# One-token attention over a long cache with a gated feed-forward branch: 28 of 32 tiles put into a hardware loop

## The chip, the cores and the metric

The kernel runs on one core of one Trainium2 chip, as one program without any work on the host. The metric is the device time of that program in microseconds (us); less is better. Timed runs of the kernel before agree within 0.13 us.

## The reference

A decode step: four sequences of one token each, 32 heads of 128, a cache of 4096 keys and values for each head, all in float32.

```
g = sigmoid(sum(x * gate_w))                       # x: 4 x 512, one gate for each sequence
q = x @ wq                                         # 4 x (32 heads x 128)
p = softmax(q . k_cache / sqrt(128))               # k_cache: 4 x 32 x 4096 x 128
a = (p . v_cache) @ wo                             # v_cache as k_cache; wo: 4096 x 512
b = (gelu(x @ w_gate) * (x @ w_up)) @ w_down       # 512 x 1792, 1792 x 512
out = g * a + (1 - g) * b                          # 4 x 512
```

The two caches are 268 MB each; each of their elements is used once.

## The kernel before

The 128 pairs of sequence and head are cut into 32 tiles of four heads of one sequence. Tile `i` has group `g = i // 4` (which four heads) and sequence `b = i % 4`. A tile's keys, K(i), are 128 partitions x 16384 elements, 8.4 MB: 32 partitions for each head, each with 128 keys of 128 elements. Its values, V(i), have the same layout. In the large SBUF buffer `big`, two K places overlap by a quarter of a tile (`RO` rows), and there is one V place; the last V goes to a K place.

All loads are issued by SP, in the order of the program, into one hardware queue. For each tile in a Python loop over `i`, fully unrolled, the order written by hand (`manual_schedule`, the program order is kept on each engine) is:

- DVE: `products(i, True)` and `sums(i, True)` work on the quarter of K(i) that the next K tile will overwrite ("shared"). Then SP may issue K(i+1).
- DVE: `products(i, False)` and `sums(i, False)` on the other three quarters. `products` multiplies K in place with the queries spread over the partitions (`QB`), `sums` adds up 128 elements for each score.
- PE: `pv(i-1)`, 32 matrix products of the weights `PM` of the tile before with V(i-1), into `PO`. Then SP may issue V(i).
- `max_a(i)`: DVE takes the maximum of each partition (L226), PE transposes the column to a row (L228).
- In the next tile, between its shared products and sums, `soft_max(i)`: DVE reduces the row to one maximum for each head (L233), PE spreads it to all partitions with a product with ones (L235), ACT copies it with a scale (L237), and four exponentials on ACT (L240) write `PM` and the row sums `RS`.
- At every fourth tile `gather` collects the four tiles' outputs with matrix products, and `weigh` divides by the row sums and writes to `ONA` with each head's values repeated four times (L300). After 16 tiles, `turn` transposes (L307) and `turned` masks and adds; the same for the second half at the end.
- `q_spread(g)` makes `QB` for a group by four matrix products, one for each head, with a column of `hmask` (L196), once in four tiles.

The gate and the first two products of the feed-forward branch run under tile 0. Behind the last tile SP loads `w_down` and `wo` (in eight pieces), and PE multiplies `wo` by the attended values as the pieces land. `SC` (scores), `m1`, `nb`, `RS` and `QB` have two buffers each.

Of the kernel before, what the change touches and what calls it, by code (L numbers as in the profile page):

```python
# [9 lines left out]
F32 = mybir.dt.float32  # L10
AF = mybir.ActivationFunctionType
OP = mybir.AluOpType
AX = mybir.AxisListType
# [4 lines left out]
def tile_gated_mix(ctx: ExitStack, tc: tile.TileContext, x, kc, vc, wq, wo, w_gate, w_up, w_down, gate_w, out):  # L18
    nc = tc.nc
    P = 128  # L20
    B, H, S, D = kc.shape
    DM = x.shape[2]
# [3 lines left out]
    HT = 4  # L26
# [10 lines left out]
    HW = 16  # L37
    E = HW * D // P
    GW = HW // HT
    WO_END = ((0, E // 2, E), (0, 4, 8, 11, 13, 15, E))  # L40
    scale = 1.0 / math.sqrt(D)
    c_gelu = math.sqrt(2.0 / math.pi)
# [23 lines left out]
    def place(a, n):  # L66
        return big[:, a:a + n]

    def K(i):
        return place(KB_ * (i % 2), TW)  # L70

    def V(i):
        return place(VA if i < NT - 1 else 0, TW)

    def load_kv(src, i, dst):
        nc.sync.dma_start(dst, src[i % B, HT * (i // B):HT * (i // B) + HT].rearrange("h (p r) d -> (h p) (r d)", p=PH))

    def load_k(i):
        load_kv(kc, i, K(i))

    def load_v(i):
        load_kv(vc, i, V(i))

    def load_f(s):
        nc.sync.dma_start(place((F0, F1)[s], KC * F), (w_gate, w_up)[s].rearrange("(p c) n -> p (c n)", c=KC))
# [14 lines left out]
    load_k(0)  # L100
    gw = consts.tile([P, KC], F32)
    nc.sync.dma_start(gw, gate_w.rearrange("(p c) -> p c", c=KC))

# [11 lines left out]

    PZ = RJ * HT
    PM = consts.tile([P, PZ + R // RJ * 32], F32)
    RS = [consts.tile([P, B, HT], F32, name=f"rs{j}") for j in range(2)]
    for t in [PM] + RS:
        nc.vector.memset(t, 0.0)  # L120


    xT_ps = ps2.tile([P, KC, B], F32, name="sm")
# [46 lines left out]
    hmask = consts.tile([P, 4, HG], F32)  # L170
# [4 lines left out]
    nc.vector.tensor_reduce(bmask, m16.rearrange("p (j b) -> p b j", b=B), axis=AX.X, op=OP.add)  # L175
    nc.vector.tensor_reduce(pmask, m16.rearrange("p (g h) -> p h g", h=HT), axis=AX.X, op=OP.add)
    nc.vector.tensor_reduce(amask, ident.rearrange("p (m a) -> p a m", a=HG), axis=AX.X, op=OP.add)
    nc.vector.tensor_reduce(hmask, ident.rearrange("p (j b a) -> p j a b", j=4, b=B), axis=AX.X, op=OP.add)
    u = place(VA - 4 * DM, 2 * DM).rearrange("p (s n) -> p s n", s=2)
    qd = place(VA - DM, D)  # L180
    for s in range(2):
# [5 lines left out]
                            op=OP.mult)  # L187


    QB = {}  # L190

    def q_spread(g):
        ps = ps1.tile([P, B, D], F32, name="q")
        for h in range(HT):
            j, a = divmod(HT * g + h, HG)
            nc.tensor.matmul(ps[h * PH:(h + 1) * PH].rearrange("p b d -> p (b d)"),  # L196
                             hmask[:, j, a:a + 1].to_broadcast([P, PH]), QM.rearrange("p b d -> p (b d)"),
                             start=True, stop=True)
        QB[g] = work.tile([P, B, D], F32, name="qb")
        nc.scalar.activation(QB[g], ps, AF.Copy)  # L200


    SC = {}

    def rows(i, shared):

        return ((R - RO, R), (0, R - RO))[not shared] if i % 2 == 0 else ((0, RO), (RO, R))[not shared]

    def products(i, shared):
        g, b = divmod(i, B)  # L210
        r0, r1 = rows(i, shared)
        t = K(i).rearrange("p (r d) -> p r d", d=D)[:, r0:r1]
        nc.vector.tensor_tensor(t, t, QB[g][:, b:b + 1, :].to_broadcast([P, r1 - r0, D]), op=OP.mult)  # L213

    def sums(i, shared):
        if shared:
            SC[i] = work.tile([P, R], F32, name="sc")
        r0, r1 = rows(i, shared)
        nc.vector.tensor_reduce(SC[i][:, r0:r1], K(i).rearrange("p (r d) -> p r d", d=D)[:, r0:r1], axis=AX.X, op=OP.add)  # L219


    MT = {}

    def max_a(i):
        m1 = work.tile([P, 1], F32, name="m1")
        nc.vector.tensor_reduce(m1, SC[i], axis=AX.X, op=OP.max)  # L226
        MT[i] = ps2.tile([1, P], F32, name="sm")
        nc.tensor.transpose(MT[i], m1, ident)  # L228

    def soft_max(i):  # L230
        g, b = divmod(i, B)
        m2 = work.tile([1, HT], F32, name="m2")
        nc.vector.tensor_reduce(m2, MT[i].rearrange("o (h p) -> o h p", h=HT), axis=AX.X, op=OP.max)  # L233
        nbp = ps2.tile([P, HT], F32, name="sm")
        nc.tensor.matmul(nbp, ones[:1, :], m2, start=True, stop=True)  # L235
        nb = work.tile([P, HT], F32, name="nb")
        nc.scalar.activation(nb, nbp, AF.Copy, scale=-scale)  # L237
        for h in range(HT):
            s = slice(h * PH, (h + 1) * PH)
            nc.scalar.activation(PM[:, PZ:].rearrange("p (c m) -> p c m", m=32)[s, :, h:RJ * HT:HT],  # L240
                                 SC[i][s, :].rearrange("p (c j) -> p c j", j=RJ), AF.Exp, bias=nb[s, h:h + 1], scale=scale,
                                 accum_out=RS[g % 2][s, b, h:h + 1])


    acc = ps1.tile([P, C4], F32, name="acc")
# [18 lines left out]
        nc.scalar.activation(t, wide, AF.Copy)  # L264
        project(stack, t, True, False)

    def pv(i):
        b = i % BP
        N, n = RJ * D, R // RJ
        for j in range(n):  # L270
            c, m0 = j % 4, PZ + 32 * j - RJ * HT * b
            nc.tensor.matmul(PO[i // BP % 2][32 * c:32 * c + 32].rearrange("p j d -> p (j d)"), PM[:, m0:m0 + 32],  # L272
                             V(i)[:, j * N:(j + 1) * N], start=b == 0 and j < 4, stop=b == BP - 1 and j >= n - 4)

    O, OS, OT = {}, {}, {}

    def gather_a(i):
        O[i // BP] = work.tile([P, RJ, D], F32, name="o")  # L280
        nc.scalar.activation(O[i // BP], PO[i // BP % 2], AF.Copy)  # L281

    def gather(g):
        OS[g] = ps2.tile([B * HT, D + 1], F32, name="sm")
        N = B // BP
        for n in range(N):
            m0 = BP * HT * (1 - n)
            for j in range(RJ):
                nc.tensor.matmul(OS[g][:, :D], sel[:, j, m0:m0 + B * HT], O[N * g + n][:, j, :],  # L289
                                 start=(n, j) == (0, 0), stop=(n, j) == (N - 1, RJ - 1))  # L290
        nc.tensor.matmul(OS[g][:, D:], RS[g % 2].rearrange("p b h -> p (b h)"), ones[:, :1], start=True, stop=True)  # L291

    ONA = consts.tile([B * HT, E, GW, HT, D // E], F32)

    def weigh(g):
        ri = work.tile([B * HT, 1], F32, name="ri")
        nc.vector.reciprocal(ri, OS[g][:, D:])  # L299
        nc.vector.tensor_scalar(ONA[:, :, g % GW], OS[g][:, :D].rearrange("p (k e) -> p e k", e=E)[:, :, None, :]  # L300
                                .to_broadcast([B * HT, E, HT, D // E]), ri, None, op0=OP.mult)


    def turn(w):
        OT[w] = ps1.tile([P, E, B * HT], F32, name="oT")
        for e in range(E):
            nc.tensor.transpose(OT[w][:, e], ONA[:, e].rearrange("q g h k -> q (g h k)"), ident[:B * HT, :B * HT])  # L307
# [47 lines left out]

    load_f(0)
    load_f(1)
    q_spread(0)
    for i in range(NT):
        g, b = divmod(i, B)  # L360
        products(i, True)
        if i > 0:
            soft_max(i - 1)
        if i > B and b == 1 and g % GW == 0:
            turned(g // GW - 1)
        sums(i, True)
        if i < NT - 1:
            load_k(i + 1)
        else:
            load_v(i)  # L370
        products(i, False)
        if i == 0:
            half, gmask = gates()
            ffn_up(0)
            ffn_up(1)
            ffn_gelu()
            load_v(0)
        sums(i, False)
        if i > 0:
            pv(i - 1)  # L380
            if i < NT - 1:
                load_v(i)
            if i % BP == 0:
                gather_a(i - 1)
            if b == 0:
                gather(g - 1)
        max_a(i)
        if i > 0 and b == 0:
            weigh(g - 1)
            if g % GW == 0:  # L390
                turn(g // GW - 1)
        if b == 1 and g + 1 < NG:
            q_spread(g + 1)
    load_d()
    load_w(0)
    load_w(1)
    spread(0)
    soft_max(NT - 1)
    pv(NT - 1)
    gather_a(NT - 1)  # L400
    gather(NG - 1)
    weigh(NG - 1)
    ffn_down()
    turn(1)
    turned(1)
# [31 lines left out]
```

## Time and profile before

| what | value |
|---|---|
| median of three timed runs | 1313.58 us (1313.56 to 1313.69) |
| span of the profiled execution, first to last instruction | 1311.7 us |
| time of the profiled execution outside its span | not listed; the timed median lies 1.9 us above the span |
| instructions | 6366 |
| busy share: PE, DVE, ACT | 30%, 87%, 7% |
| data moved | 565 MB at a mean of 431 GB/s |
| mean granted TensorE clock | 0.633 |

In the rows of the profile that are shown below, a line such as `L213` is a line of the kernel before, and `out<-in` names the buffers. In a timeline row the first number is the start in us from the start of the span, the second the duration in us; in square brackets stand the idle time of that engine just ahead and what ended it. In a row of a group the numbers behind the bar are busy time in us, the mean duration of one in ns, and again the idle time ahead. `SPq` rows are the issues of transfers. A matrix product in float32 appears as two records, so the 32 products of `pv` are shown as 64.

### The profile page before, as it was taken

What the parts mean: (1) busy time and instruction counts of PE and PEld (TensorE: products, weight loads), DVE (VectorE), ACT (ScalarE), POOL (GpSimd) and SP (SyncE); (2) the same over time, 40 slices, a digit from 0 to 9 for tenths busy, and PEclk for the clock granted to TensorE, in tenths of its full rate; (3) what the DMA queues carried; (4) which work ended last, traced back from release to release, by engine and by line L of the source; (5) the groups of instructions that cost most, each with busy time, mean ns of one, the idle gap of its engine ahead of it and who ended that gap; (6) DMA issues with size and microseconds to landing.
All of it is one profiled execution on the core that took longest, in us unless ns stands there. A gap on an engine that the chain in (4) does not pass through costs nothing.

```text
span 1311.7 us, 6366 instructions
## 1 busy us (share of the span) xinstructions
PE 392.2 (30%) x2728; PEld 131.1 (10%) x2728; DVE 1143.1 (87%) x261; ACT 92.6 (7%) x321; POOL 0.7 (0%) x6
## 2 busy tenths in 40 slices
PE   2403323322233221333232233322133333123237
PEld 0100001000010000100001000100001000010013
DVE  1899889988899988988989988998889898898890
ACT  0010000000000100000000000000000000000010
POOL 0000000000000000000000000000000000000000
PEclk9656666556666655666656666665566665566669
DMA  9999999999999999999999999999999999999998
GB/s 416 436 428 442 422 440 426 438 436 436 436 428 436 432 436 436 436 430 432 434 436 434 436 430 436 428 438 430 434 446 422 442 422 442 434 434 440 426 426 341
DMA packets 11143, 565.07 MB, mean 431 GB/s; under 512 B 1368, under 2 KB 1384, under 8 KB 1900
## 3 DMA queue, kind: packets, MB, share of 16 engines
q1 hardware_dynamic: 11116, 564.68, 99.5%
q8 instruction: 21, 0.34, 0.1%
q14 instruction: 6, 0.05, 0.0%
HBM read 564.67 MB, written 0.01 MB: 430 GB/s over the span
## 4 chain that ended last, share of the span: by engine, by line
DMA 73%; DVE 26%; issue 0%; PE 0%; SPq 0%; ACT 0%; DVEq 0%
DMA big<-in_A_k_cache 69%; DVE big L213 13%; DVE sc L219 13%; DMA big<-in_A_v_cache 2%; DMA big<-in_A_wo 2%; DVE m L233 0%; DVE hT L349 0%; PE acc L259 0%; DVE big L346 0%; DVE big L345 0%; DVE big L341 0%; DVE big L343 0%; ACT big L344 0%; DVE m L226 0%; DVE t L313 0%
## 5 line engine op out<-in xcount | busy, mean ns | idle before, releaser
L213 DVE TENSOR_TENSOR big<-big,qb 128x4096 f32<-128x4096 f32 x64 | 555.8, 8685 | 104.1 <-DMA big<-in_A_k_cache 104.1
L219 DVE TENSOR_REDUCE sc<-big 128x32 f32<-128x4096 f32 x64 | 555.4, 8678 | 1.1
L272 PE MATMUL po<-big,PM 128*32 128x512 f32 x2048 | 295.1, 741 | 437.2 <-DMA big<-in_A_v_cache 434.8
L272 PEld LDWEIGHTS po<-big,PM 128*32 128x32 f32 x2048 | 80.9, 133 | 625.2 <-issue 622.7
L235 PE MATMUL sm<-m,ones 1*128 1x4 f32 x64 | 18.7, 360 | 218.0 <-DVE m L233 218.0
L228 PE MATMUL sm<-ident,m 128*1 128x128 f32 x32 | 11.7, 365 | 214.5 <-DVE m L226 182.7
L240 ACT ACTIVATE PM<-sc,nb 32x128 f32<-32x128 f32 x128 | 67.3, 526 | 2.5
L237 ACT ACTIVATE nb<-sm 128x4 f32<-128x4 f32 x32 | 5.5, 173 | 570.3 <-PE sm L235 570.3
L235 PEld LDWEIGHTS sm<-m,ones 1*128 1x128 f32 x64 | 15.9, 306 | 237.7 <-DVE m L233 237.7
L281 ACT ACTIVATE o<-po 128x512 f32<-128x512 f32 x16 | 9.6, 597 | 324.8 <-PE po L272 324.8
L228 PEld LDWEIGHTS sm<-ident,m 128*1 128x1 f32 x32 | 2.5, 79 | 237.0 <-issue 185.9
L240 ACT ACTIVATION_READ_ACCUMULATOR PM<-sc,nb 32x1 f32 x128 | 26.2, 205 | 0.0
L200 ACT ACTIVATE qb<-q 128x512 f32<-128x512 f32 x8 | 4.8, 597 | 245.3 <-PE q L196 245.3
L128 DVE COPY xT<-sm 128x128 f32<-128x128 f32 x4 | 0.9, 284 | 20.6 <-PE sm L125 20.6
L196 PE MATMUL q<-QM,hmask 128*32 128x512 f32 x64 | 14.6, 1004 | 3.5 <-DVE QM L186 3.5
L289 PE MATMUL sm<-o,sel 128*16 128x128 f32 x128 | 15.6, 273 | 0.0
L334 PE MATMUL q<-big,xT 128*32 128x448 f32 x64 | 10.3, 810 | 9.4 <-DMA big<-in_B_w_gate 4.9
L299 DVE RECIPROCAL ri<-sm 16x1 f32<-16x1 f32 x8 | 1.2, 146 | 13.3 <-PE sm L291 13.3
L289 PEld LDWEIGHTS sm<-o,sel 128*16 128x16 f32 x128 | 11.8, 97 | 7.4 <-issue 5.0
L413 DVE COPY res<-acc 128x128 f32<-128x128 f32 x1 | 0.3, 291 | 12.7 <-PE acc L259 12.7
L226 DVE TENSOR_REDUCE m<-sc 128x1 f32<-128x128 f32 x32 | 9.2, 286 | 1.1
L233 DVE TENSOR_REDUCE m<-sm 1x4 f32<-1x128 f32 x32 | 8.7, 272 | 0.6 <-PE sm L228 0.6
(61 smaller groups left out, 77.1 us busy)
## 6 DMA issues: line engine op xcount, KB each, us to landing
big<-in_A_wo SPq DMA_DIRECT2D x2, 2048.0 KB, 27.0
big<-in_B_w_gate SPq DMA_DIRECT2D x1, 3584.0 KB, 21.4
big<-in_B_w_up SPq DMA_DIRECT2D x1, 3584.0 KB, 27.5
big<-in_B_w_down SPq DMA_DIRECT2D x1, 3584.0 KB, 18.0
big<-in_A_wo SPq DMA_DIRECT2D x2, 1024.0 KB, 24.6
big<-in_A_wo SPq DMA_DIRECT2D x2, 512.0 KB, 28.2
big<-in_A_wo SPq DMA_DIRECT2D x1, 768.0 KB, 28.0
big<-in_A_k_cache SPq DMA_DIRECT2D x32, 29.6
```

What stands on the lines that cost most here:

```text
L196: nc.tensor.matmul(ps[h * PH:(h + 1) * PH].rearrange("p b d -> p (b d)"), hmask[:, j, a:a + 1].to_broadcast([P, PH]), QM.rearrange("p b d ...
L213: nc.vector.tensor_tensor(t, t, QB[g][:, b:b + 1, :].to_broadcast([P, r1 - r0, D]), op=OP.mult)
L219: nc.vector.tensor_reduce(SC[i][:, r0:r1], K(i).rearrange("p (r d) -> p r d", d=D)[:, r0:r1], axis=AX.X, op=OP.add)
L226: nc.vector.tensor_reduce(m1, SC[i], axis=AX.X, op=OP.max)
L228: nc.tensor.transpose(MT[i], m1, ident)
L233: nc.vector.tensor_reduce(m2, MT[i].rearrange("o (h p) -> o h p", h=HT), axis=AX.X, op=OP.max)
L235: nc.tensor.matmul(nbp, ones[:1, :], m2, start=True, stop=True)
L240: nc.scalar.activation(PM[:, PZ:].rearrange("p (c m) -> p c m", m=32)[s, :, h:RJ * HT:HT], SC[i][s, :].rearrange("p (c j) -> p c j", j=RJ) ...
L272: nc.tensor.matmul(PO[i // BP % 2][32 * c:32 * c + 32].rearrange("p j d -> p (j d)"), PM[:, m0:m0 + 32], V(i)[:, j * N:(j + 1) * N], start ...
L281: nc.scalar.activation(O[i // BP], PO[i // BP % 2], AF.Copy)
L289: nc.tensor.matmul(OS[g][:, :D], sel[:, j, m0:m0 + B * HT], O[N * g + n][:, j, :], start=(n, j) == (0, 0), stop=(n, j) == (N - 1, RJ - 1))
L334: nc.tensor.matmul(ps[32 * j:32 * j + 32, :], xT[:, c, :32], place((F0, F1)[s] + c * F + j * FG, FG), start=c == 0, stop=c == KC - 1)
```

## The change

Tile 0 is run ahead of the loop. Tiles 1 to 28 run in a hardware loop of seven turns on all engines: one turn is four slots, `b` = 1, 2, 3 and 0, the last of them the first tile of the next group. Tiles 29 to 31 are unrolled after it. Each engine counts the turns in a register, computes from it the addresses and the values of semaphores that it waits for, and branches back. There is no barrier between turns. Behind the loop, in the built program, SP waits until the semaphores of all eight load lanes and of PE, ACT and DVE have the values of the last turn, all engines meet in one barrier, POOL clears the loop's eleven semaphores, and the code after the loop begins.

Other edits that come with it:

- The maxima stay on DVE: the column of partition maxima is repeated over 32 columns and transposed in 32x32 blocks, and reduced again with a changed sign. `soft_max(b)` follows `sums(b, False)` in the same slot. The factor 1/sqrt(128) is put into the queries (`bmask`), so that the exponentials use a scale of 1.
- The queries are spread by one matrix product with `hcur`, a copy of four columns of `hmask`, each 32 times, that DVE writes once a turn (`q_pick`).
- `SC`, `m1`, `nb`, `RS` and `QB` have one buffer each.
- `gather` writes the first seven groups to `ON`; `expand` repeats them behind the loop. `expand(0)`, `turn(0)` and `turned(0)` stand behind tile 31, ahead of `pv(31)`.

```diff
-    def load_kv(src, i, dst):
-        nc.sync.dma_start(dst, src[i % B, HT * (i // B):HT * (i // B) + HT].rearrange("h (p r) d -> (h p) (r d)", p=PH))
+    def load_kv(src, g, b, dst):
+        nc.sync.dma_start(dst, src[b, bass.ds(g * HT, HT)].rearrange("h (p r) d -> (h p) (r d)", p=PH))
...
+    nc.vector.tensor_scalar(bmask, bmask, scale, None, op0=OP.mult)
...
+    def q_pick(g):
+        nc.vector.tensor_scalar(hcur, hmask[:, bass.ds(g * HT, HT), None].to_broadcast([P, HT, PH]), 1.0, None, op0=OP.mult)
+
+    def q_spread():
         ps = ps1.tile([P, B, D], F32, name="q")
-        for h in range(HT):
-            j, a = divmod(HT * g + h, HG)
-            nc.tensor.matmul(ps[h * PH:(h + 1) * PH].rearrange("p b d -> p (b d)"),
-                             hmask[:, j, a:a + 1].to_broadcast([P, PH]), QM.rearrange("p b d -> p (b d)"),
-                             start=True, stop=True)
-        QB[g] = work.tile([P, B, D], F32, name="qb")
-        nc.scalar.activation(QB[g], ps, AF.Copy)
+        nc.tensor.matmul(ps.rearrange("p b d -> p (b d)"), hcur.rearrange("p h k -> p (h k)"),
+                         QM.rearrange("p b d -> p (b d)"), start=True, stop=True)
+        nc.scalar.activation(QB, ps, AF.Copy)
...
+    def soft_max(b):
+        nc.vector.tensor_reduce(m1, SC, axis=AX.X, op=OP.max)
+        nc.vector.transpose(mt, m1.to_broadcast([P, PH]))
+        nc.vector.tensor_reduce(nb, mt, axis=AX.X, op=OP.max, negate=True)
         for h in range(HT):
             s = slice(h * PH, (h + 1) * PH)
             nc.scalar.activation(PM[:, PZ:].rearrange("p (c m) -> p c m", m=32)[s, :, h:RJ * HT:HT],
-                                 SC[i][s, :].rearrange("p (c j) -> p c j", j=RJ), AF.Exp, bias=nb[s, h:h + 1], scale=scale,
-                                 accum_out=RS[g % 2][s, b, h:h + 1])
+                                 SC[s, :].rearrange("p (c j) -> p c j", j=RJ), AF.Exp, bias=nb[s], scale=1.0,
+                                 accum_out=RS[s, b, h:h + 1])
...
+        if last:
+            nc.vector.tensor_scalar(OX[:, :, GW - 1], q[:, :, None].to_broadcast([B * HT, E, HT, D // E]), ri, None,
+                                    op0=OP.mult)
+        else:
+            nc.vector.tensor_scalar(ON[:, bass.ds(g, 1)], q[:, None], ri, None, op0=OP.mult)
+
+    def expand(w):
+        for n in range(GW):
+            if w * GW + n < NG - 1:
+                nc.vector.tensor_copy(OX[:, :, n], ON[:, w * GW + n, :, None, :].to_broadcast([B * HT, E, HT, D // E]))
...
+    def slot(g, b, last=False):
+        c = (b - 1) % B
+        gn = g + 1 if b == 0 else g
+        if b == 1:
+            q_pick_next(g)
+        products(b, True)
+        sums(b, True)
+        if not last:
+            load_k(gn if b < B - 1 else g + 1, (b + 1) % B)
         else:
-            load_v(i)
...
+            load_v(g, b, True)
+        products(b, False)
+        sums(b, False)
+        pv(c)
+        if not last:
+            load_v(gn, b)
+        if c % BP == BP - 1:
+            gather_a(c // BP)
+        if b == 0:
+            gather(g)
+        if b == B - 1:
+            q_spread()
+        soft_max(b)
...
+    with tc.For_i(0, NL, iteration_sync="reg_based") as g:
+        for b in (1, 2, 3, 0):
+            slot(g, b)
+    q_pick_next = lambda g: None
+    for b in range(1, B):
+        slot(NG - 1, b, b == B - 1)
     load_d()
     load_w(0)
     load_w(1)
+    expand(0)
+    turn(0)
+    turned(0)
     spread(0)
-    soft_max(NT - 1)
-    pv(NT - 1)
-    gather_a(NT - 1)
-    gather(NG - 1)
-    weigh(NG - 1)
+    expand(1)
+    pv(B - 1, True)
+    gather_a(1)
+    gather(NG - 1, True)
     ffn_down()
```

More of the change, by code (lines that the diff above doesn't have):

```diff
@@ L39, in tile_gated_mix @@
     GW = HW // HT
+    NL = NG - 1
     WO_END = ((0, E // 2, E), (0, 4, 8, 11, 13, 15, E))
@@ L67, in place, with K, V, load_k @@
         return big[:, a:a + n]
[L69 to L73, printed above, removed]
-    def load_kv(src, i, dst):
[L76 to L82, printed above, removed]
+    def K(b):
+        return place(KB_ * (b % 2), TW)
+    def V(last):
+        return place(0 if last else VA, TW)
+    def load_kv(src, g, b, dst):
+        nc.sync.dma_start(dst, src[b, bass.ds(g * HT, HT)].rearrange("h (p r) d -> (h p) (r d)", p=PH))
+    def load_k(g, b):
+        load_kv(kc, g, b, K(b))
+    def load_v(g, b, last=False):
+        load_kv(vc, g, b, V(last))
     def load_f(s):
@@ L99, in tile_gated_mix @@
     nc.sync.dma_start(x_sb, x.rearrange("b s d -> (b s) d"))
-    load_k(0)
+    load_k(0, 0)
     gw = consts.tile([P, KC], F32)
@@ L117, in tile_gated_mix @@
     PM = consts.tile([P, PZ + R // RJ * 32], F32)
-    RS = [consts.tile([P, B, HT], F32, name=f"rs{j}") for j in range(2)]
-    for t in [PM] + RS:
-        nc.vector.memset(t, 0.0)
+    RS = consts.tile([P, B, HT], F32)
+    nc.vector.memset(PM, 0.0)
+    nc.vector.memset(RS, 0.0)
     xT_ps = ps2.tile([P, KC, B], F32, name="sm")
@@ L169, in tile_gated_mix @@
     amask = consts.tile([P, HG], F32)
-    hmask = consts.tile([P, 4, HG], F32)
+    hmask = consts.tile([P, H], F32)
+    hcur = consts.tile([P, HT, PH], F32)
     pmask = consts.tile([P, HT], F32)
@@ L175, in tile_gated_mix @@
     nc.vector.tensor_reduce(bmask, m16.rearrange("p (j b) -> p b j", b=B), axis=AX.X, op=OP.add)
+    nc.vector.tensor_scalar(bmask, bmask, scale, None, op0=OP.mult)
     nc.vector.tensor_reduce(pmask, m16.rearrange("p (g h) -> p h g", h=HT), axis=AX.X, op=OP.add)
     nc.vector.tensor_reduce(amask, ident.rearrange("p (m a) -> p a m", a=HG), axis=AX.X, op=OP.add)
-    nc.vector.tensor_reduce(hmask, ident.rearrange("p (j b a) -> p j a b", j=4, b=B), axis=AX.X, op=OP.add)
+    nc.vector.tensor_reduce(hmask.rearrange("p (j a) -> p j a", j=4), ident.rearrange("p (j b a) -> p j a b", j=4, b=B),
+                            axis=AX.X, op=OP.add)
     u = place(VA - 4 * DM, 2 * DM).rearrange("p (s n) -> p s n", s=2)
@@ L187, in tile_gated_mix @@
                             op=OP.mult)
-    QB = {}
-    def q_spread(g):
+    QB = consts.tile([P, B, D], F32)
+    def q_pick(g):
+        nc.vector.tensor_scalar(hcur, hmask[:, bass.ds(g * HT, HT), None].to_broadcast([P, HT, PH]), 1.0, None, op0=OP.mult)
+    def q_spread():
         ps = ps1.tile([P, B, D], F32, name="q")
-        for h in range(HT):
-            j, a = divmod(HT * g + h, HG)
-            nc.tensor.matmul(ps[h * PH:(h + 1) * PH].rearrange("p b d -> p (b d)"),
-                             hmask[:, j, a:a + 1].to_broadcast([P, PH]), QM.rearrange("p b d -> p (b d)"),
-                             start=True, stop=True)
-        QB[g] = work.tile([P, B, D], F32, name="qb")
-        nc.scalar.activation(QB[g], ps, AF.Copy)
@@ L203, in tile_gated_mix @@
[L203 to L219, printed above, removed]
@@ L222, in tile_gated_mix @@
[L222 to L237, printed above, removed]
+        nc.tensor.matmul(ps.rearrange("p b d -> p (b d)"), hcur.rearrange("p h k -> p (h k)"),
+                         QM.rearrange("p b d -> p (b d)"), start=True, stop=True)
@@ new lines, in q_spread, with rows, products, sums @@
+        nc.scalar.activation(QB, ps, AF.Copy)
+    SC = consts.tile([P, R], F32)
+    def rows(b, shared):
+        return ((R - RO, R), (0, R - RO))[not shared] if b % 2 == 0 else ((0, RO), (RO, R))[not shared]
+    def products(b, shared):
+        r0, r1 = rows(b, shared)
+        t = K(b).rearrange("p (r d) -> p r d", d=D)[:, r0:r1]
+        nc.vector.tensor_tensor(t, t, QB[:, b:b + 1, :].to_broadcast([P, r1 - r0, D]), op=OP.mult)
+    def sums(b, shared):
+        r0, r1 = rows(b, shared)
+        nc.vector.tensor_reduce(SC[:, r0:r1], K(b).rearrange("p (r d) -> p r d", d=D)[:, r0:r1], axis=AX.X, op=OP.add)
@@ L238, in soft_max @@
+    m1 = consts.tile([P, 1], F32)
+    mt = consts.tile([P, PH], F32)
+    nb = consts.tile([P, 1], F32)
+    def soft_max(b):
+        nc.vector.tensor_reduce(m1, SC, axis=AX.X, op=OP.max)
+        nc.vector.transpose(mt, m1.to_broadcast([P, PH]))
+        nc.vector.tensor_reduce(nb, mt, axis=AX.X, op=OP.max, negate=True)
         for h in range(HT):
@@ L265, in fold, with pv, gather_a, gather @@
         project(stack, t, True, False)
-    def pv(i):
-        b = i % BP
+    def pv(b, last=False):
         N, n = RJ * D, R // RJ
         for j in range(n):
[L271 to L284, printed above, removed]
+            c, m0 = j % 4, PZ + 32 * j - RJ * HT * (b % BP)
+            nc.tensor.matmul(PO[b // BP][32 * c:32 * c + 32].rearrange("p j d -> p (j d)"), PM[:, m0:m0 + 32],
+                             V(last)[:, j * N:(j + 1) * N], start=b % BP == 0 and j < 4, stop=b % BP == BP - 1 and j >= n - 4)
+    O = [consts.tile([P, RJ, D], F32, name=f"o{n}") for n in range(B // BP)]
+    def gather_a(n):
+        nc.scalar.activation(O[n], PO[n], AF.Copy)
+    ON = consts.tile([B * HT, NG - 1, E, D // E], F32)
+    OX = place(ES + 2 * E * 32 + DM, E * GW * HT * D // E)[:B * HT].rearrange("q (e g h k) -> q e g h k", e=E, g=GW, h=HT)
+    ri = consts.tile([B * HT, 1], F32)
+    def gather(g, last=False):
+        os_ = ps2.tile([B * HT, D + 1], F32, name="sm")
         N = B // BP
@@ L288, in gather @@
             for j in range(RJ):
-                nc.tensor.matmul(OS[g][:, :D], sel[:, j, m0:m0 + B * HT], O[N * g + n][:, j, :],
+                nc.tensor.matmul(os_[:, :D], sel[:, j, m0:m0 + B * HT], O[n][:, j, :],
                                  start=(n, j) == (0, 0), stop=(n, j) == (N - 1, RJ - 1))
[L291 to L301, printed above, removed]
+        nc.tensor.matmul(os_[:, D:], RS.rearrange("p b h -> p (b h)"), ones[:, :1], start=True, stop=True)
+        nc.vector.reciprocal(ri, os_[:, D:])
+        q = os_[:, :D].rearrange("q (k e) -> q e k", e=E)
+        if last:
[7 more added lines that the diff above has]
+                nc.vector.tensor_copy(OX[:, :, n], ON[:, w * GW + n, :, None, :].to_broadcast([B * HT, E, HT, D // E]))
+    OT = {}
     def turn(w):
@@ L306, in turn @@
         for e in range(E):
-            nc.tensor.transpose(OT[w][:, e], ONA[:, e].rearrange("q g h k -> q (g h k)"), ident[:B * HT, :B * HT])
+            nc.tensor.transpose(OT[w][:, e], OX[:, e].rearrange("q g h k -> q (g h k)"),
+                                ident[:B * HT, :B * HT])
     def turned(w):
@@ L357, in tile_gated_mix, with q_pick_next @@
     load_f(1)
[L358 to L368, printed above, removed]
-        else:
-            load_v(i)
[L371 to L393, printed above, removed]
+    q_pick(0)
+    q_spread()
+    products(0, True)
+    sums(0, True)
+    load_k(0, 1)
+    products(0, False)
+    half, gmask = gates()
+    ffn_up(0)
+    ffn_up(1)
+    ffn_gelu()
+    load_v(0, 0)
+    sums(0, False)
+    soft_max(0)
+    def slot(g, b, last=False):
[7 more added lines that the diff above has]
+            load_k(gn if b < B - 1 else g + 1, (b + 1) % B)
+        else:
+            load_v(g, b, True)
[9 more added lines that the diff above has]
+        if b == B - 1:
+            q_spread()
+        soft_max(b)
+    def q_pick_next(g):
+        q_pick(g + 1)
+    with tc.For_i(0, NL, iteration_sync="reg_based") as g:
[4 more added lines that the diff above has]
+        slot(NG - 1, b, b == B - 1)
     load_d()
```

## The prediction

> **What bounds the kernel now.** I read the page first: its forty slices, the queues and the chain that ended last.
>
> ```profile
> DMA  9999999999999999999999999999999999999998
> GB/s 416 436 428 442 422 440 426 438 436 436 436 428 436 432 436 436 436 430 432 434 436 434 436 430 436 428 438 430 434 446 422 442 422 442 434 434 440 426 426 341
> q1 hardware_dynamic: 11116, 564.68, 99.5%
> q8 instruction: 21, 0.34, 0.1%
> DMA 73%; DVE 26%; issue 0%; PE 0%; SPq 0%; ACT 0%; DVEq 0%
> ```
>
> The transfers are busy in every slice but the last, at a rate that hardly moves: the kernel is bound by the bytes of its one load queue. The chain gives 26% to DVE, which tempts one to save DVE time. Whether that share is real is read from one tile in the timeline (start, duration, engine, line). I take tile 28 and the start of tile 29, where the change puts the end of its loop.
>
> ```profile
> 1134.37 0.33 SPq L76 DMA_DIRECT2D big<-in_A_k_cache  x1
> 1154.47 0.33 SPq L76 DMA_DIRECT2D big<-in_A_v_cache  x1
> 1163.99 4.43 DVE L213 TENSOR_TENSOR big<-big,qb 128x4096 f32<-128x4096 f32 x1 [2.63 <-DMA big<-in_A_k_cache]
> 1168.53 4.41 DVE L219 TENSOR_REDUCE sc<-big 128x32 f32<-128x4096 f32 x1
> 1172.97 0.33 SPq L76 DMA_DIRECT2D big<-in_A_k_cache  x1
> 1183.40 9.08 PE L272 MATMUL po<-big,PM 128*32 128x512 f32 x64 [14.16 <-DMA big<-in_A_v_cache]
> 1192.54 0.33 SPq L76 DMA_DIRECT2D big<-in_A_v_cache  x1
> 1202.71 4.42 DVE L213 TENSOR_TENSOR big<-big,qb 128x4096 f32<-128x4096 f32 x1 [3.60 <-DMA big<-in_A_k_cache]
> ```
>
> K(29) is issued at 1134.37 and V(28) at 1154.47. They land in the order of issue, 19.4 us apart: K(29) starts DVE at 1163.99, V(28) starts PE at 1183.40, K(30) starts DVE at 1202.71. Each issue comes well before the queue runs dry. K(30) is issued at 1172.97, 10.4 us before V(28) lands; V(29) at 1192.54, 10.2 us before K(30) lands. So the DVE pieces in the chain are covered: an issue that comes up to 10 us later costs nothing. What costs time is a gap in the queue.
>
> ```profile
> 165.59 0.33 SPq L76 DMA_DIRECT2D big<-in_A_k_cache  x1
> 1211.68 0.33 SPq L76 DMA_DIRECT2D big<-in_A_k_cache  x1
> 83.24 4.42 DVE L213 TENSOR_TENSOR big<-big,qb 128x4096 f32<-128x4096 f32 x1
> 98.74 8.69 PE L272 MATMUL po<-big,PM 128*32 128x512 f32 x64 [10.27 <-DMA big<-in_A_v_cache]
> 118.26 4.42 DVE L213 TENSOR_TENSOR big<-big,qb 128x4096 f32<-128x4096 f32 x1
> ```
>
> The first two rows are the issues of K(4) and K(31), 27 tiles apart: 38.74 us a tile. The two DVE rows are tiles 1 and 2, where K had long landed and DVE ran without a pause: 35.02 us a tile. DVE has 3.7 us a tile to spare. (The PE row, V(0)'s landing, is for the start, below.)
>
> **Part 1: inside the loop.** The loads keep their bytes, layout and order. DVE loses the reduction of the transposed maxima (L233) and gains a 32x32 transpose and a reduction of 32 columns; once per turn it also writes the 128x128 head selector (`hcur`).
>
> ```profile
> L233 DVE TENSOR_REDUCE m<-sm 1x4 f32<-1x128 f32 x32 | 8.7, 272 | 0.6 <-PE sm L228 0.6
> L349 DVE STREAM_TRANSPOSE hT<-big 128x32 f32<-128x32 f32 x14 | 1.7, 192 | 0.0
> L175 DVE TENSOR_REDUCE bmask<-m 128x4 f32<-128x16 f32 x1 | 0.2, 178 | 0.0
> L128 DVE COPY xT<-sm 128x128 f32<-128x128 f32 x4 | 0.9, 284 | 20.6 <-PE sm L125 20.6
> L300 DVE TENSOR_SCALAR ONA<-sm,ri 16x512 f32<-16x512 f32 x8 | 5.9, 738 | 0.3
> L213 DVEq EVENT_SEMAPHORE  x1: 21/21/21, 42.0 to 42.0; - x1
> L219 DVE TENSOR_REDUCE sc<-big 128x96 f32<-128x12288 f32 x32 | 414.5, 12952 | 1.1
> L213 DVE TENSOR_TENSOR big<-big,qb 128x12288 f32<-128x12288 f32 x32 | 414.2, 12945 | 0.0
> L240 ACT ACTIVATE PM<-sc,nb 32x128 f32<-32x128 f32 x128 | 67.3, 526 | 2.5
> L240 ACT ACTIVATION_READ_ACCUMULATOR PM<-sc,nb 32x1 f32 x128 | 26.2, 205 | 0.0
> ```
>
> Nearest rows: +0.19 for the transpose, +0.18 for the reduction, +0.28/4 for the selector, -0.27: +0.17 us a tile, so 35.2. The unrolled kernel had nearly no register work. The built loop body holds 68 DVE instructions, 31 of them arithmetic; the other 37, 9.2 a slot, compute registers or wait. No row shows a register operation. Bounds: 0.021 us each (the semaphore row) to 0.33 us (SP's load issue), so 0.2 to 3.1 us a slot; I take the low end, as most are of the semaphore's sort and can run under an operation of 13 us. Even the high end gives 38.3, under 38.74. PE and ACT work is shorter or equal (four query matmuls become one; the maxima's transpose, broadcast and copy go). `soft_max` now ends the slot, and its four exponentials need at most 4 x (0.53 + 0.21) = 2.9 us: they end before the next tile's `sums` overwrites the one score buffer, some 8 us on. **Sum inside the loop: 0**, covered by the queue; from below, at most 3.9 us could be won, 27 tiles x (38.74 - 38.60), if every tile took only what tile 28 took (1134.37 to 1172.97).
>
> [...] The trace before has no branch; its instruction queue (q8) moved 0.34 MB with no engine waiting. [...]
>
> **Part 2: the loop's end.** The built program does not flow from turn 7 into tile 29. Behind its last load, V(28), SP waits until all eight load semaphores have their final value, V(28)'s landing included; then all engines meet in a barrier, and only then comes tile 29. Queued behind that wait on SP are K(30) and V(29); behind the barrier, DVE's products of tile 29 and PE's pv(28). Before, K(29) started DVE at 1163.99; now nothing starts until V(28) has landed, 1183.40, with an empty queue.
>
> ```profile
> 0.34 0.10 POOL L426 MEMSET const-uint8-127<- 128x1 uint8 x1
> 0.83 0.17 DVE L106 MEMSET ones<- 128x128 f32 x1 [0.83 <-PEq L426]
> 1309.04 0.66 SPq L414 DMA_DIRECT2D out<-res  x1
> big<-in_A_wq SPq DMA_DIRECT2D x1, 21.9
> ```
>
> - Barrier. The nearest row is the barrier that opens the program: POOL's last memset ends at 0.44, DVE starts at 0.83, 0.4 us. The exit has two such hops and clears eleven semaphores: I take 1.0. Bounds 0.4 and 2.7 (from the output's issue at 1309.04 to the span's end, 1311.7, a store, its landing and the closing barrier together). DVE starts tile 29 at 1184.4.
> - Issue of K(30): after the shared products and sums, 1163.99 to 1172.97, 8.98 us: 1193.4. V(29) follows pv(28), 9.1 us after the barrier: 1193.5, right behind it.
> - Landing of K(30). In a full queue a load takes 19.4; the one load issued to an empty queue, wq, with the same bytes, took 21.9 from issue to landing. K(30) lands at 1215.3, against 1202.7: **+12.6 us**. The cost of starting is between 0 (19.4) and 2.5.
>
> [...]
>
> Afterwards the queue is full again. DVE at 35.3 a tile starts tile 30 at 1219.7 and tile 31 at 1255.0, so K(31) is issued at 1228.7, before V(29) lands at 1234.7, and V(31) at 1264.0, before V(30) lands at 1273.4. V(31) lands at 1292.7. The lost time is not won back: the bytes bound.
>
> **Part 3: the tail.** Expanding and turning the first half moves behind tile 31.
>
> ```profile
> 1279.97 27.61 DMA big<-in_A_wo
> 1280.35 8.39 PE L272 MATMUL po<-big,PM 128*32 128x512 f32 x64 [2.45 <-ACT PM L240]
> 1293.94 1.16 PE L307 MATMUL oT<-ident,ONA 16*128 16x16 f32 x16
> 1298.36 1.92 PE L254 MATMUL wide<-big 128*32 128x512 f32 x16 [1.40 <-DMA big<-in_A_wo]
> 1303.23 1.08 PE L259 MATMUL acc<-big 128*32 128x128 f32 x32 [0.94 <-DMA big<-in_A_wo]
> 1305.06 0.86 PE L259 MATMUL acc<-big 128*32 128x128 f32 x24 [0.75 <-DMA big<-in_A_wo]
> 1306.26 0.65 PE L259 MATMUL acc<-big 128*32 128x128 f32 x16 [0.34 <-DMA big<-in_A_wo]
> 1307.62 1.03 PE L259 MATMUL acc<-big 128*32 128x128 f32 x24 [0.72 <-DMA big<-in_A_wo]
> ```
>
> Tile 31's maxima are ready near 1290.6; four copies of at most 0.74 (L300's row) and sixteen transposes of 1.16 in all stand on PE ahead of pv(31), which starts near 1295.1. Shifted by 12.6 it would have started at 1293.0: 2.1 us late. PE waits for wo pieces by 1.40 + 0.94 + 0.75 + 0.34 + 0.72 = 4.2 us after that, so the last piece still ends the kernel. **Sum: 0**; copies at twice the price make pv(31) 5.1 late, 0.9 us at the end.
>
> The start: K(2), the tightest issue, has 6.5 us of cover (issued 8.96 after tile 1's 83.24; V(0) lands at 98.7). `q_pick` and the entry's register writes fit in it.
>
> **Sum.** Span 1311.7 + 12.6 = 1324.3. The timed runs lie 1.9 above the span (median 1313.58), so 1313.58 + 12.6 = **1326.2 us**.
>
> **Rivals.**
> - **A, not slower: the exit passes early.** If SP's waits were met by an older count, K(30) would be issued as now; the barrier's 1.0 us would vanish in the 10.4 of cover, and the time would be 1313.6, or as low as 1309.7 with the 3.9 of part 1. It decides if K(30) is issued before V(28) lands. Against it: the registers step by 16 a turn and the semaphores start at 16, so the exit's value is met by the seventh V load alone.
> - **B: DVE becomes the bound.** From 0.38 us for a register operation on, a slot exceeds 38.74. At 0.5 it is 39.8, 1.1 x 28 = 31 us more: 1357. For it: nothing shows such an operation. Against it: 34.7 of the 35 us are four long operations (twice 4.4, twice 12.95), under which they can run.
> [...]
>
> **How the numbers follow.** Forecast 0.86; A 0.06 (two thirds without a change, one third faster), B 0.04, C 0.04. A difference under 0.2%, 2.6 us, can't be told from none. Slower: 0.86 + 0.08 = 0.94; same 0.04; faster 0.02. Range: low end, barrier 0.4 and the 3.9 won inside the loop, 12.6 - 0.6 - 3.9 = +8.1: 1321.7. High end, barrier 2.7, tail 0.9 and DVE over the bound by 0.15 us a tile (4.2): 12.6 + 1.7 + 0.9 + 4.2 = +19.4: 1333.0. A, B and C at full size stay outside, 0.14 in all.
>
> **What would show it.** Right: K issues 38.6 to 38.8 us apart through the loop; one gap in the transfers of about 12.6 us, with SP waiting for a V load before it and DVE's shared products first after it; DVE back to back at tile 30; the last wo piece still ending the chain. [...]

## The result and the profile after

| | before | changed |
|---|---|---|
| median of the timed runs | 1313.63 us | 1324.79 us |
| ratio to before, 95% interval | | 1.0083 [1.0072, 1.0095] |
| profiled execution: its time, its span | not listed, 1311.7 us | 1324.56 us, 1322.5 us |

The change makes the kernel 11.2 us slower; 12.6 was forecast. Three parts of the page of the changed kernel answer to those shown of before: the forty slices of transfers, what they moved, and the queues.

```profile
DMA  9999999999999999999999999999999999969998
GB/s 413 443 418 438 439 432 430 438 440 424 436 444 420 440 440 420 440 440 428 434 438 440 424 436 444 420 440 440 420 440 440 428 434 438 440 267 412 444 426 353
q1 hardware_dynamic: 11116, 564.68, 98.7%
q8 instruction: 7, 0.11, 0.0%
```

The bytes are the same. There is one hole, in the 36th slice (267 GB/s, 6 tenths busy): the loop's end. Elsewhere the rate is as before. Something else changed that I had not weighed: 7 instruction fetches instead of 21.

The hole in the timeline of the changed kernel (start, duration, engine, line; tile 28 and on):

```profile
1132.02 0.33 SPq L77 DMA_DIRECT2D big<-in_A_k_cache  x1
1151.46 0.33 SPq L77 DMA_DIRECT2D big<-in_A_v_cache  x1
1181.54 4.42 DVE L215 TENSOR_TENSOR big<-big,QB 128x4096 f32<-128x4096 f32 x1 [22.60 <-SPq L444]
1181.69 9.77 PE L263 MATMUL po<-big,PM 128*32 128x512 f32 x64 [28.50 <-SPq L444]
1190.52 0.34 SPq L77 DMA_DIRECT2D big<-in_A_k_cache  x1
1191.52 0.34 SPq L77 DMA_DIRECT2D big<-in_A_v_cache  x1
1217.05 4.42 DVE L215 TENSOR_TENSOR big<-big,QB 128x4096 f32<-128x4096 f32 x1
1231.86 8.59 PE L263 MATMUL po<-big,PM 128*32 128x512 f32 x64 [40.40 <-DMA big<-in_A_v_cache]
1252.55 4.41 DVE L215 TENSOR_TENSOR big<-big,QB 128x4096 f32<-128x4096 f32 x1
```

K(29) and V(28) are issued as ever. Then DVE stands for 22.60 us and PE for 28.50, both released by SP, and K(30) is issued 39.06 us after V(28), where before it was 18.50. What SP itself waited for at the loop's line:

```profile
SPq L397 <- DMA big<-in_A_v_cache: 19.3, 1, 19.3
SPq L397 <- DMA big<-in_A_k_cache: 9.2, 1, 9.2
```

It waited through K(29)'s landing and then 19.3 us for V(28)'s. That is the exit.

For the next steps the landings are needed themselves. The trace holds, for each load, when each of its 16 DMA engines reported; "landed" is the last report, "spread" the time from the first to the last (us):

```
              before             changed
load       landed  spread     landed  spread
V(0)        98.61    1.7       99.12    2.0
V(28)     1183.27    4.4     1180.86    1.9
K(30)     1202.68    4.5     1212.40    0.7
V(31)     1279.95    4.5     1291.08    2.0
last wo   1308.19    4.6     1318.99    1.8
```

So the 10.8 us between the two spans fall into three parts. Up to V(28) the changed kernel is **2.4 ahead**. From V(28) to K(30) it needs 31.5 us where the kernel before needs 19.4: **12.1 lost**. From there to the last piece of wo another **1.1** is lost. -2.4 + 12.1 + 1.1 = 10.8.

### The profile page after: what moved, and what is told of

Same layout as the page of the kernel before. It is cut to its first block, busy times and chain, and to the rows that moved or that the text cites. A ratio compares the mean times of both kernels' runs of the same rounds, so it can differ in the third digit from the quotient of the medians.

```text
span 1322.5 us, 6803 instructions
## 1 busy us (share of the span) xinstructions
PE 356.4 (27%) x2586; PEld 113.7 (9%) x2586; DVE 1153.1 (87%) x308; ACT 87.6 (7%) x290; POOL 0.7 (0%) x6
## 5 line engine op out<-in xcount | busy, mean ns | idle before, releaser
L215 DVE TENSOR_TENSOR big<-big,QB 128x4096 f32<-128x4096 f32 x64 | 555.9, 8686 | 99.1 <-DMA big<-in_A_k_cache 76.4
L219 DVE TENSOR_REDUCE SC<-big 128x32 f32<-128x4096 f32 x64 | 555.9, 8686 | 4.5
L232 ACT ACTIVATE PM<-SC,nb 32x128 f32<-32x128 f32 x128 | 67.2, 525 | 479.1 <-DVE nb L229 476.4
L232 ACT ACTIVATION_READ_ACCUMULATOR PM<-SC,nb 32x1 f32 x128 | 26.1, 204 | 0.0
L203 ACT ACTIVATE QB<-q 128x512 f32<-128x512 f32 x9 | 5.4, 597 | 272.7 <-PE q L201 272.7
L201 PE MATMUL q<-QM,hcur 128*128 128x512 f32 x18 | 10.2, 648 | 3.6 <-DVE hcur L197 3.6
L227 DVE TENSOR_REDUCE m<-SC 128x1 f32<-128x128 f32 x32 | 9.0, 281 | 0.9
L165 PE MATMUL po<-big,xT 128*32 128x512 f32 x64 | 8.4, 684 | 0.4 <-DVE xT L129 0.4
L228 DVE STREAM_TRANSPOSE mt<-m 128x32 f32<-128x32 f32 x32 | 6.8, 211 | 1.6
L229 DVE TENSOR_REDUCE nb<-mt 128x1 f32<-128x32 f32 x32 | 6.0, 186 | 1.1
## 6 DMA issues: line engine op xcount, KB each, us to landing
big<-in_B_w_down SPq DMA_DIRECT2D x1, 3584.0 KB, 19.3
```

The source lines that it names most:

```text
L165: nc.tensor.matmul(PO[s][32 * j:32 * j + 32].rearrange("p j d -> p (j d)"), xT[:, c, :32], w[:, n0:n0 + HB * D], start=c == 0, stop=c == K ...
L201: nc.tensor.matmul(ps.rearrange("p b d -> p (b d)"), hcur.rearrange("p h k -> p (h k)"), QM.rearrange("p b d -> p (b d)"), start=True, sto ...
L215: nc.vector.tensor_tensor(t, t, QB[:, b:b + 1, :].to_broadcast([P, r1 - r0, D]), op=OP.mult)
L219: nc.vector.tensor_reduce(SC[:, r0:r1], K(b).rearrange("p (r d) -> p r d", d=D)[:, r0:r1], axis=AX.X, op=OP.add)
L227: nc.vector.tensor_reduce(m1, SC, axis=AX.X, op=OP.max)
L228: nc.vector.transpose(mt, m1.to_broadcast([P, PH]))
```

## The experiments

**The loop against the other edits.** The Python loop in place of the hardware loop, all else as changed:

```diff
-    with tc.For_i(0, NL, iteration_sync="reg_based") as g:
+    for g in range(NL):
         for b in (1, 2, 3, 0):
             slot(g, b)
```

> The changed kernel with its loop unrolled again: all other edits stay (maxima on DVE, one query product, single buffers, first half expanded and turned in the tail). Theory: the loop's end alone costs the time (V(29) lands 9.7 us later than before, of which the gap is 12.1 and the loop's faster spacing gives back 2.4 to 2.8), so without the loop 1313.6, between 1313 and 1315, with no gap in the transfers, and the spacing of K loads again near 38.74 with some 17 instruction fetches. Rival 1: the other edits brought the faster spacing; then about 1311, spacing 38.64. Rival 2: the other edits cost time in the tail or in the slots; then above 1316.

Measured: 1313.61 us, ratio 0.9999 [0.9991, 1.0008]. Its page:

```profile
span 1311.7 us, 6100 instructions
q8 instruction: 20, 0.33, 0.1%
```

The whole difference is the loop's. Maxima on DVE, the single query product, the single buffers and the expansion in the tail cost and bring nothing that can be measured, and the fetches are back.

**The place of the cut.** The next tile's shared products and sums moved to the end of a turn:

```diff
+    def head(b):
+        products(b, True)
+        sums(b, True)
...
     def slot(g, b, last=False):
...
-        products(b, True)
-        sums(b, True)
...
         soft_max(b)
+        if not last:
+            head((b + 1) % B)
...
+    head(1)
     with tc.For_i(0, NL, iteration_sync="reg_based") as g:
```

> The changed kernel with the loop's cut moved by one step: the shared products and sums of the next tile stand at the end of a turn, so that K(30) can be issued right behind the barrier. Theory: of the 12.1 us at the exit, 9.0 are the shared products and sums that stand between barrier and issue, 0.6 the barrier, 2.5 the start into an empty queue. So 9.0 less than the changed kernel: 1315.8, between 1315 and 1317; K(30) is issued 0.6 to 0.8 us after V(28) has landed. Rival: the exit costs its 12 us wherever it is cut (code behind the loop to be fetched, counters to be cleared); then 1324.8.

Measured: 1316.36 us, ratio 1.0020 [1.0011, 1.0029]. Its timeline at the exit; V(28) landed at 1180.88:

```profile
1181.53 12.96 DVE L215 TENSOR_TENSOR big<-big,QB 128x12288 f32<-128x12288 f32 x1 [10.99 <-PEq L449]
1181.97 0.34 SPq L77 DMA_DIRECT2D big<-in_A_k_cache  x1
```

DVE now stands 11.0 us instead of 22.6, and K(30) is issued 1.1 us after the landing instead of 9.7. The exit's cost is set by what must run between its barrier and the first load. The 0.6 over my figure is a balance. K(30) was issued 0.4 us later after the landing than I had taken and needed 23.2 us from issue to landing, not 21.9, with a spread of 2.0; two 16 KB fetches of the code behind the loop (1182.7 and 1188.9) fell into it. From K(30) to the end this version lost nothing against the kernel before, where the changed kernel lost 1.1. This version is 8.4 us better than the changed kernel and still slower than before.

**Two exits.**

```diff
-    with tc.For_i(0, NL, iteration_sync="reg_based") as g:
-        for b in (1, 2, 3, 0):
-            slot(g, b)
+    for g0, g1 in ((0, 4), (4, NL)):
+        with tc.For_i(g0, g1, iteration_sync="reg_based") as g:
+            for b in (1, 2, 3, 0):
+                slot(g, b)
```

> The changed kernel with two loops, of four and of three turns, so with two exits. Theory: each exit empties the queue and costs about 12.1 us, so 1324.8 + 12.1 = 1336.9, between 1336 and 1339, with two gaps in the transfers. Rival: the time is lost once, in the start of the unrolled end part and the tail, and a second exit costs only its barrier, 0.6 us, hidden under the queue: 1325.5.

Measured: 1339.3 us, ratio 1.0193 [1.0179, 1.0208], 14.5 above the changed kernel, a little more than the range. What DVE waited for at the two exits (sum, times, longest):

```profile
DVE hcur L197 <- PEq L398: 23.7, 1, 23.7
DVE big L215 <- PEq L445: 23.6, 1, 23.6
```

Its timeline, the issues of K(17) and V(16), the start of tile 17 and the issue of K(18):

```profile
668.12 0.33 SPq L77 DMA_DIRECT2D big<-in_A_k_cache  x1
688.27 0.33 SPq L77 DMA_DIRECT2D big<-in_A_v_cache  x1
719.03 4.43 DVE L215 TENSOR_TENSOR big<-big,QB 128x4096 f32<-128x4096 f32 x1
728.22 0.34 SPq L77 DMA_DIRECT2D big<-in_A_k_cache  x1
```

Two stands of DVE, two holes. V(16) landed at 716.95, and the products began 2.1 us later, against 0.7 at the other kind of exit: behind this barrier the second loop's registers are set and the query columns picked first. From V(16) to K(18) it is 33.1 us, 13.8 more than the 19.3 of a full queue; the second exit costs 12.1 more. The rest of the excess is a spacing of up to 19.46 between landings behind the first exit, which I did not explain, and one fetch (at 1172.3, in an interval of 20.3).

**The wait alone, without a loop.** In the kernel before, one copy on DVE that needs V(28):

```diff
         g, b = divmod(i, B)
+        if i == 29:
+            seen = consts.tile([P, 1], F32, name="seen")
+            nc.vector.tensor_copy(seen, place(VA, 1))
         products(i, True)
```

> The unrolled kernel before with one wait and no loop: ahead of tile 29's shared products DVE copies one column of V(28), so that it waits until V(28) has landed. Theory: this wait is what the loop's exit costs: V(28) lands at 1183.3, K(30) is issued 9.3 us later into an empty queue and needs 21.9, so it lands at 1214.5 instead of 1202.7: +11.8, less up to 3 for the spread that the empty queue wipes out (4.4 us there): 1324, between 1322 and 1326. Rival: barrier, counters and code behind the loop make a good part of the 12: then 1320 or less.

Measured: 1326.43 us, ratio 1.0097 [1.0082, 1.0112]: slower than the changed kernel. Timeline, DVE's copy, the issue of K(30), and V(29)'s arrival at PE:

```profile
1183.43 0.15 DVE L363 COPY seen<-big 128x1 f32<-128x1 f32 x1 [21.92 <-DMA big<-in_A_v_cache]
1192.46 0.33 SPq L76 DMA_DIRECT2D big<-in_A_k_cache  x1
1233.87 8.35 PE L272 MATMUL po<-big,PM 128*32 128x512 f32 x64 [10.10 <-DMA big<-in_A_v_cache]
```

One wait in the wrong place costs 12.8 us, 0.4 above my range; the loop is not needed for it. V(29) comes 41.4 us after K(30)'s issue, as in the changed kernel (1190.52 to 1231.86, 41.3). The reduction that I expected from a wiped-out spread did not come; my reading, which no run isolates, is that a landing is the slowest engine's, and that one too stood empty until K(30) was issued.

**The control: late, but into a full queue.** Two more reductions on DVE ahead of tile 29:

```diff
         g, b = divmod(i, B)
+        if i == 29:
+            spare = consts.tile([P, RO], F32, name="spare")
+            for _ in range(2):
+                nc.vector.tensor_reduce(spare, K(i).rearrange("p (r d) -> p r d", d=D)[:, :RO], axis=AX.X, op=OP.add)
         products(i, True)
```

> The control for the wait alone: the kernel before with two reductions more on DVE ahead of tile 29's shared products (8.8 us), so that K(30) is issued about as late after the start of tile 29 as the wait's own products cost, but while V(28) is still under way (1181.8 against its landing at 1183.3). Theory: an issue that comes up to 10 us later is free while the queue holds a load: 1313.6, within 0.5. Rival: DVE's pieces in the chain count (26% of it by the page): up to 8.8 more, 1322.

Measured: 1316.17 us, ratio 1.0019 [1.0010, 1.0028]: neither free nor 8.8. A miss, and a useful one.

```profile
1181.92 0.33 SPq L76 DMA_DIRECT2D big<-in_A_k_cache  x1
1183.44 9.58 PE L272 MATMUL po<-big,PM 128*32 128x512 f32 x64 [5.25 <-DMA big<-in_A_v_cache]
1224.31 9.63 PE L272 MATMUL po<-big,PM 128*32 128x512 f32 x64 [11.08 <-DMA big<-in_A_v_cache]
```

K(30) was issued 1.4 us before V(28) landed (1183.30), and V(29) reached PE 2.2 us later than before (1222.11). In these runs a load of 8.4 MB landed 21.9 us after its issue to an empty queue, and 19.3 after the load ahead of it in a full one. If the later of the two decides, my estimate, an issue must come 2.6 us before that landing to be free, and K(30), 1.2 us short of this, should have landed at 1203.8; it landed at 1204.8, with a fetch in it at 1188.5 and a spread of 1.7. I put the missing 1.0 down to the fetch, which is argued and not shown. The cover of a K issue is then 10.4 - 2.6 = 7.8 us, not 10; if all 2.1 us of K(30)'s delay (1202.68 before) came from the late issue, it is 6.8.

**Where the 2.4 us come from: instruction fetches.** First try, 64 small products with a row of ones a tile on PE in the kernel before:

```diff
             if i < NT - 1:
                 load_v(i)
+                for _ in range(64):
+                    nc.tensor.matmul(wide[:, :4], ones[:1, :], ones[:1, :4], start=True, stop=True)
```

> The kernel before with 64 tiny matrix products more on PE after each tile's issue of V (1x128 by 1x4, into a buffer that is written anew later): 31 x 64 x 4 = 7936 PE instructions more, some 31 instruction fetches of 16 KB, on an engine that is idle then (PE waits 14 us a tile). Theory: what the loop wins inside (38.64 for 38.74 us a tile) is instruction fetches, which pass through the DMA engines of the loads: each delays one engine by about 0.9 us, a load has landed when its slowest engine has, and the spread between the first and the last engine grows (0.7 to 4.6 us over 17 fetches before). With 31 more: 3 to 8 us longer, 1317 to 1322, with a spread of 8 to 12. Rival: fetches are harmless, and the loop's spacing comes from something else (loads with a register address, fewer PE instructions); then 1313.6, within 0.5.

Measured: 1432.31 us, ratio 1.0901 [1.0864, 1.0938]. Inconclusive: the products were not cheap. Their group, and DVE's longest sum of waiting:

```profile
L384 PE MATMUL wide<-ones 1*128 1x4 f32 x3840 | 726.3, 324 | 0.0
```

```profile
DVE m L233 <- PE sm L228: 123.5, 24, 11.5
```

23 us a tile made PE late, DVE waited for its maxima, the loads were issued late, and the queue ran dry again and again. With transposes of a third of the price:

```diff
             if b == 0:
                 gather(g - 1)
+            if i < NT - 1:
+                for _ in range(96):
+                    nc.tensor.transpose(wide[:, :16], ones[:16, :], ident[:16, :16])
```

> The kernel before with 96 small transposes more on PE (16x16, some 0.07 us each, so 7 us a tile where PE waits 14) behind each tile's products with V, into a buffer that is written anew later: 30 x 96 x 2 = 5760 PE instructions more, some 22 instruction fetches of 16 KB, without making PE the bound. Theory: fetches pass through the loads' DMA engines and delay single ones by up to 0.9 us; 17 of them raised the spread between the first and the last engine from 0.7 to 4.6 us in the kernel before; 22 more raise it by 3 to 6 and the time with it: 1317.5, between 1316 and 1320. Rival: fetches are harmless and the loop's closer spacing comes from elsewhere: 1313.6, within 0.5.

Measured: 1317.97 us, ratio 1.0033 [1.0021, 1.0045]. From its page, and the groups of the filler and of DVE's products:

```profile
span 1316.0 us, 12126 instructions
q8 instruction: 44, 0.72, 0.2%
```

```profile
L389 PE MATMUL wide<-ident,ones 16*128 16x16 f32 x2880 | 227.0, 226 | 0.0
L213 DVE TENSOR_TENSOR big<-big,qb 128x4096 f32<-128x4096 f32 x64 | 555.8, 8685 | 107.3 <-DMA big<-in_A_k_cache 107.3
```

While the tiles run, DVE's products wait for K alone, 107.3 us against 104.1, so PE's extra work does not hold them up; yet 23 more fetches go with 4.3 us, 0.19 each. The spread at V(31) is 7.5 us.

The 0.19 is an average of unequal steps. From one landing to the next the queue takes 19.3 us, but 20.4 in two intervals of the kernel before (with the fetches at 605.3 and 1109.0) and in five of this one (305.9, 541.5, 772.4, 1008.0 and 1241.3): at every eighth fetch, 1.1 us each, with the spread growing by 1.0. The three more make 3.3 of the 4.3 us; behind the other fetches an interval is at most 0.3 longer in these two runs.

And the same transposes inside the loop:

```diff
         if b == 0:
             gather(g)
+        if not last:
+            for _ in range(96):
+                nc.tensor.transpose(wide[:, :16], ones[:16, :], ident[:16, :16])
         if b == B - 1:
             q_spread()
```

> The changed kernel with the same 96 transposes a tile inside its loop: a turn of PE grows from some 560 to some 1330 instructions, and 5184 of the additional ones are executed from the loop. Theory: the loop's code stays resident, so hardly any fetch is added (one or two behind the loop): the changed kernel's 1324.8, within 1.0, with a spread near 1.9 in the loop. Rival: a body of this size is fetched anew at each back edge: 25 to 30 fetches more, 1328 or above, with steps of the spread once a turn.

Measured: 1325.28 us, ratio 1.0086 [1.0072, 1.0100], against 1324.79 of the changed kernel.

```profile
span 1324.0 us, 12563 instructions
q8 instruction: 12, 0.20, 0.1%
```

The same instructions are executed, twice as many as before, with 12 fetches. Their times in the trace: three up to 142 us, two at 182 and 194, still in the first turn, then none until 1184. From the second turn on nothing is fetched, and the spread stands still at 2.8 us. I had expected one or two fetches more than in the changed kernel and a spread of 1.9; it is five more, three of them ahead of V(28), which lands 1.1 us later (1181.96). The filler itself costs next to nothing here, 0.5 us in all, so the 4.3 us of the unrolled version are not PE's work: the number of fetches, not of instructions, moves the time.

## Why the prediction was right, point by point

The exit was priced at 12.6 us and cost 12.1, with each of its steps close to its row. The 2.4 won ahead of it and the 1.1 lost behind it were not forecast; that they partly cancel, and so leave the total near the forecast, is luck.

- **What bounds the kernel.** Right in the main: bytes through one queue. But a gap is not all that lengthens it, as the fetches show. The unrolled version shows that work off that path is worth nothing here.
- **Cover of 10 us.** Wrong in size: the control shows that an issue 8.9 us later is not free, and 21.9 against 19.3 us gives 7.8. The step left out the 2.6 us by which, as estimated there, an issue must come ahead of the landing before it. It did not enter the sum, as no issue in the loop came near it.
- **Inside the loop, 0.** The mis-sized term: 2.4 us were won by V(28), within the 3.9 that I had as a bound and as the low end of the range, without a cause. The cause is fewer instruction fetches; that they cost the loads time is shown by the two light fillers. Up to V(28)'s landing the kernel before has 17 fetches, the changed one 2. The two intervals of 20.4 us, together 2.2 too long, stand in the kernel before; from V(0) to V(28) the changed one has none. That each fetch holds up a single DMA engine is argued from the spread alone. DVE's part was near: 35.6 us a slot in the loop where K had long landed (85.15 to 120.76) for 35.2, and 36.6 in a turn's last slot, with `gather` and the back edge (195.74 to 232.38, where the wait for K begins); both are under 38.74. The rows of DVE for the first two tiles of the loop, the new operations as groups, a register operation from the rows of one line (shortest, median, longest in ns), and what DVE waited for:

```profile
85.15 4.43 DVE L215 TENSOR_TENSOR big<-big,QB 128x4096 f32<-128x4096 f32 x1
120.76 4.41 DVE L215 TENSOR_TENSOR big<-big,QB 128x4096 f32<-128x4096 f32 x1
```

```profile
L228 DVE STREAM_TRANSPOSE mt<-m 128x32 f32<-128x32 f32 x32 | 6.8, 211 | 1.6
L229 DVE TENSOR_REDUCE nb<-mt 128x1 f32<-128x32 f32 x32 | 6.0, 186 | 1.1
```

```profile
L215 DVEq ALU_OP  x7: 40/40/58, 84.8 to 1004.9; - x7
```

```profile
DVE big L215 <- DMA big<-in_A_k_cache: 76.4, 27, 6.3
DVE hcur L197 <- DVE nb L229: 3.0, 6, 0.5
```

- **Barrier, 1.0.** 0.7, from V(28)'s landing at 1180.86 to DVE at 1181.54.
- **Issue of K(30), 8.98 behind the barrier.** 8.98 (1181.54 to 1190.52). V(29) was 1.0 behind it rather than 0.1, as pv(28) took 9.8; K(30) covered that.
- **Landing, 21.9 from issue.** 21.88. The bare row of wq was the right price, 2.6 us over a full queue. 0.7 + 9.0 + 2.6 = 12.3, against 12.6.
- **Afterwards and tail, 0.** 1.1 was lost. Behind the exit the 16 DMA engines run level again (spread 0.7), and the fetch at 1277.1, in V(31)'s transfer, set the spread back to 2.0 and V(31) 1.4 late; 0.3 of it came back by the last wo piece. In the wait alone it is the same: a fetch at 1278.9, and V(31) 1.2 late. The expansion was cheaper than bounded (0.35 us a copy), and PE stood for the wo pieces as forecast:

```profile
1288.04 1.41 DVE L296 COPY big<-ON 16x512 f32<-16x512 f32 x4
1291.32 9.57 PE L263 MATMUL po<-big,PM 128*32 128x512 f32 x64
1318.44 1.01 PE L251 MATMUL acc<-big 128*32 128x128 f32 x24 [0.60 <-DMA big<-in_A_wo]
```

- **Rivals.** A fell with SP's wait of 19.3 us for V(28). B fell with DVE's idle time: 76 us of waiting for K remain, and a register operation (the ALU_OP row) takes 0.04 us, about a tenth of what B needed; one began at 89.8 under a reduction of 4.42 us that began at 89.7 (L219). C, a fetch at each back edge that waits behind the loads, was an assumption of mine, and no run shows DVE standing for one: at the six back edges DVE lost 3.0 us in all, 0.5 each, between its last reduction and the next turn's first operation (the `hcur` row), and with the transposes inside the loop even a PE turn of some 1330 instructions was not fetched again. In straight code no row shown has an engine waiting for a fetch; the loads paid 0.19 us for each (light filler).
- No version beat the kernel before. By these rows the best cut still pays barrier and issue 1.1, an empty queue's start 2.6 and fetches behind the loop 1.3, together 5.0, against the 2.4 that the loop gives.

## What to carry to other kernels

In a kernel that is bound by one queue of loads, price a loop by its exit: find the last load issued inside, see what must run between its landing and the next issue, and put the cut where that is nothing; here moving it by one step took 8.4 of 11.2 us away. An engine's share of the chain that ended last did not price a delay here (DVE had 26%, and 8.9 us more on it cost 2.5); count the cover from the issue to the landing ahead of it, less the start of a transfer (2.6 us here). Between turns and in its arithmetic this loop cost the kernel nothing.

## What the runs showed of the hardware

- An instruction fetch of 16 KB cost a full load queue 0.19 us on average (23 more: 4.3 us), though DVE's products wait for K alone: 1.1 us at every eighth in the kernel before and with the light filler, at most 0.3 at the others. Behind an exit, where the engines ran level, one cost 1.4 (changed kernel, V(31)). The 16 DMA engines drifted apart in the course (0.7 to 4.6 us in the kernel before, 7.7 with the filler), and an empty queue brought them level (4.0 to 0.9 in the wait alone).
- A load of 8.4 MB landed 21.9 us after its issue to an empty queue, and 19.3 after the one ahead in a full one (empty: wq, and K(30) behind the exit and behind the wait alone; with two fetches in it, 23.2).
- This loop, without a barrier between turns, cost about 0.5 us of DVE's time at a back edge and nothing of the kernel's.
